# A replayed plan that knows of a shared port: new costs, three ways for V's parts, and a new order table in an attention and feed-forward kernel

## The chip, the cores and the metric

One core of a Trainium2 chip runs the whole program in one launch. TensorE (PE) multiplies; its weight loads run beside it (PEld). VectorE (DVE), ScalarE (ACT) and GpSimd (POOL) do the elementwise work, and SyncE (SP) issues the DMAs. The metric is the device time of one execution in microseconds (us).

## The reference

```python
q, k, v: (8, 8, 576, 64) f32          # batch, heads, tokens, head dimension
scores = q @ k.T / sqrt(64)
scores = where(scores >= max(scores) - tau, scores, -1e9)      # row by row
attn = exp(scores - max); attn = attn / (sum(attn) + 1e-9)
x = (attn @ v) -> (4608 tokens, 512)
h = x @ w_in                                                  # (512, 2048)
g = where(h >= 1, h, where(h <= -1, 0, (h + 1)**2 / 4))
out = g @ w_out                                               # (2048, 512)
```

The kernel is given float64 weights and float32 q, k and v. Most products are made in f16 with each operand split in a high and a low part (hi and lo, where lo is the value less hi), so three products stand for one.

## The kernel before

**What is computed where.** Q, K and V come with the head dimension first, two heads of a batch (a pair) in one buffer. The 4608 query rows are cut into 288 tiles of 128 rows. A tile goes through this chain: scores on PE (L1073, two PSUM buffers s; the table PAIR says whether two tiles' products are issued together, J, or one tile after the other, S), row minimum on DVE (smax, L1127), exp on ACT (sexp, L1137), mask and row sum on DVE (smask, L1151), reciprocal on DVE, then the normalised row in two f16 parts, and a transposing DMA from SP (send, L1213) into eT. The parts are made in one of the ways that the table TILE names by tile: P (the default: normalise on POOL L1169, hi on ACT L1177, lo on POOL L1180), N (normalise on ACT L1172), V (hi on ACT L1207, lo on DVE L1210) and S (from PSUM). Attention times V (av, L1299) gives x on PSUM, which ACT and DVE split.

**V, Q and K.** For V of batches 1 to 7, POOL writes the high part twice (hi, L728), DVE the low part (lo, L733), and SP sends it. Q and K of the first four pairs are used plainly in f32, the others are split: by P (POOL normalises, ACT hi, POOL lo) or D (ACT hi, DVE lo, L656), which the table QHOW names by pair. The scale of V in batch 0 is taken from Gram matrices on PE (SSQV "G"), in the other batches from sums of squares on ACT (L685).

**Weights.** 16 slices each of w_in and w_out are loaded (512 KB each), turned from float64 into float32 bits (fix, low and b2 on ACT, POOL and DVE: table SIGN), measured by Gram matrices on PE (L881), scaled and split (table CONV: A and G on ACT and POOL with the low part on POOL L933; D with the low part on DVE, rest2, L939; P and Q with two PE products and one eviction, diff, L942; M one product).

**FFN.** ffn1 (L466, ph<-x,WI) makes 512 columns of h in a PSUM buffer ph (three of them), ACT and DVE make g (relu, square, gate, ghi, glo), and ffn2 (L466, acc<-WO,..) adds into the one buffer acc.

**What sets the order.** Each operation is put into a list with its engine and a cost in us written out by hand. ORDER is a table of 5016 numbers, the places of those operations in a replay (Plan.order): it gives each a time by its engine, its inputs (HOP is the time from one engine to another) and its buffers, and the operations are then issued by these times. So the table and the costs set the order in which each engine's queue stands; nothing is moved when the program runs. Where the replay leaves PE without work for over 0.4 us before 120 us, fillers are put in: products of ones into a PSUM bank that is free (keep_warm, L1454), for 75% of the gap.

Of the kernel before, what the change touches and what calls it, by code (L numbers as in the profile page):

```python
# [14 lines left out]
ALU = mybir.AluOpType  # L15
# [24 lines left out]
SEND, VSEND = (1.24, 0.2, 2.1), (1.7, 0.5, 2.5)  # L40
ORDER = [
# [219 lines left out]
class Op:  # L261
    def __init__(self, eng, cost, fn, work, mode):
        self.eng, self.cost, self.fn, self.work, self.mode = eng, cost, fn, work, mode
        self.take, self.uses, self.next, self.behind = [], [], [], []
        self.gives = None


class Plan:


    HOP = {"PE": 0.21, "DVE": 0.16, "ACT": 0.17, "POOL": 0.1, "SP": 0.08}
    FREE, QUEUE, TURN, PAUSE = 0.18, 6.5, 0.097, (3.4, 2.2)
# [56 lines left out]
    def order(self):  # L329
# [3 lines left out]
        for o in self.ops:  # L333
            o.t = 0.0
# [1176 lines left out]
```

## Time and profile before

| | |
|---|---|
| time, median of 3 runs (lowest to highest) | 1097.77 us (1097.62 to 1098.02) |
| span of the profiled execution | 1097.3 us |
| PE, DVE, ACT, POOL busy | 1073.0, 906.1, 871.2, 759.4 us |
| granted clock of PE, mean of the span | 0.993 |

The span runs from the first to the last instruction on the core; what the runs show beyond it is about 0.5 us. Busy is the time in which at least one instruction of an engine runs. The clock is a share of 2.4 GHz. An instruction's duration contains about 0.07 us that lies under the instruction before it where a queue runs without a gap.

### The profile page before, as it was taken

The page shows a single profiled execution, that of the slowest core. Times are in us where ns is not written, and L with a number is a line of the kernel's source. Part 1 is how long each engine was busy: PE and PEld are TensorE (multiplying, and loading weights), DVE is VectorE, ACT ScalarE, POOL GpSimd, SP SyncE. Part 2 cuts the span into 40 slices and gives each one's busy share as a digit, 9 for nine tenths or more (in the row PEclk, how much of TensorE's full clock was granted, in tenths as well). Part 3 has the DMA queues.
Part 4 walks back from the last instruction along what each step waited for, and adds up shares of the span by engine and source line. Part 5 has one row for each costly group of instructions (what it writes and reads, how often), then busy time and mean ns, then how long its engine had stood idle before and what let it go on. Part 6 is the DMA issues. An engine that isn't in the chain of part 4 may idle for free.

```text
span 1097.3 us, 36713 instructions
## 1 busy us (share of the span) xinstructions
PE 1073.0 (98%) x14591; PEld 790.6 (72%) x14591; DVE 906.1 (83%) x2651; ACT 871.2 (79%) x1682; POOL 759.4 (69%) x880
## 2 busy tenths in 40 slices
PE   8799999999999999999999999999999999999998
PEld 7477668777777777776777677777786677767774
DVE  5899999999888888988898998888887899877223
ACT  5999989897888897887798888778788986776333
POOL 5999998786678785897668776576567885565000
PEclk9799999999999999999999999999999999999999
DMA  9997899775977887787778788569856676557000
GB/s 352 332 256 143 139 188 141 152 140 115 191 140 141 152 152 127 135 150 137 139 142 146 150 128 147 113 127 164 151 102 120 131 128 127 105 95 132 18 15 20
DMA packets 420668, 155.88 MB, mean 142 GB/s; under 512 B 399504, under 2 KB 399504, under 8 KB 420496
## 3 DMA queue, kind: packets, MB, share of 16 engines
q1 hardware_dynamic: 420416, 153.41, 71.7%
q8 instruction: 114, 1.87, 0.7%
q14 instruction: 58, 0.48, 0.2%
q10 hardware_dynamic: 80, 0.13, 0.0%
HBM read 45.09 MB, written 9.44 MB: 50 GB/s over the span
## 4 chain that ended last, share of the span: by engine, by line
PE 80%; DVE 10%; DMA 5%; POOL 2%; issue 2%; ACT 1%; SPq 0%; DVEq 0%; POOLq 0%; ACTq 0%
PE acc L466 30%; PE ph L466 30%; PE s L1073 9%; PE ph L1299 9%; DMA eT<-hl 2%; DVE s L1127 2%; DVE e L1151 2%; POOL hl L1180 1%; PE ph L1454 1%; DMA qq<-in_q_dram 1%; DMA kk<-in_k_dram 1%; DMA raw<-in_v_dram 1%; DVE ph L1383 1%; POOL e L1169 0%; DVE WO L939 0%
## 5 line engine op out<-in xcount | busy, mean ns | idle before, releaser
L466 PEld LDWEIGHTS <-WI 128*64 128x64 f16 (+1 forms) x7446 | 407.3, 108 | 55.1 <-issue 18.3
L1180 POOL TENSOR_TENSOR hl<-e,hl 128x576 f16<-128x576 f32 x267 | 347.3, 1309 | 107.7 <-ACT hl L1177 101.8
L466 PE MATMUL ph<-x,WI 128*64 128x256 f16 (+1 forms) x6912 | 400.6, 264 | 2.3 <-DVE x L1311 0.9
L1169 POOL TENSOR_SCALAR e<-e,sm 128x576 f32<-128x576 f32 x259 | 203.5, 790 | 106.6 <-DVE sm L1161 75.3
L1151 DVE SCALAR_TENSOR_TENSOR e<-s,sm,e 128x578 f32<-128x578 f32 x286 | 229.9, 812 | 21.6 <-ACT e L1137 17.0
L1137 ACT ACTIVATE e<-s,sm 128x576 f32<-128x576 f32 x288 | 208.5, 739 | 40.4 <-DVE s L1127 36.4
L1127 DVE TENSOR_SCALAR_CACHE_REDUCE s<-s,pc 128x576 f32<-128x576 f32 x252 | 203.5, 820 | 36.6 <-PE s L1073 35.3
L1177 ACT ACTIVATE hl<-e 128x576 f16<-128x576 f32 x267 | 178.2, 680 | 44.1 <-POOL e L1169 41.1
L466 PE MATMUL acc<-WO,ga 128*64 128x512 f16 (+1 forms) x1590 | 203.4, 380 | 0.0
L1073 PE MATMUL s<-kk,qq 64*128 64x288 f16 (+3 forms) x1840 | 152.1, 300 | 9.9 <-DMA qq<-in_q_dram 5.2
L466 PEld LDWEIGHTS <-ga 128*64 128x64 f16 (+1 forms) x1590 | 91.2, 109 | 82.3 <-issue 9.9
L1383 DVE SCALAR_TENSOR_TENSOR ph<-ph,fcs,asq 128x512 f32<-128x512 f32 (+1 forms) x160 | 111.7, 700 | 46.1 <-ACT asq L1379 44.9
L1376 ACT ACTIVATE asq<-ph,fcs 128x512 f32<-128x512 f32 (+1 forms) x160 | 116.1, 736 | 37.7 <-PE ph L466 36.9
L1299 PE MATMUL ph<-eT,vst 128*64 128x320 f16 (+2 forms) x1928 | 122.7, 279 | 2.9 <-DMA eT<-hl 2.0
L1299 PEld LDWEIGHTS <-vst 128*64 128x64 f16 x1928 | 100.2, 110 | 22.9 <-issue 7.9
L1073 PEld LDWEIGHTS <-qq 64*128 64x128 f16 (+1 forms) x1680 | 66.2, 96 | 48.3 <-issue 35.6
L1388 ACT ACTIVATE ga<-ph,fcs 128x256 f16<-128x256 f32 (+1 forms) x160 | 70.2, 450 | 29.2 <-DVE ph L1383 22.4
L1379 ACT ACTIVATE asq<-asq 128x512 f32<-128x512 f32 x144 | 90.3, 629 | 3.2
L1393 DVE SCALAR_TENSOR_TENSOR ga<-ph,fcs,ga 128x256 f16<-128x256 f32 (+1 forms) x160 | 70.5, 449 | 23.7 <-ACT WI L1388 8.3
L466 PE MATMUL acc<-WO,gb 128*64 128x512 f16 (+1 forms) x546 | 71.0, 379 | 0.0
L466 PE MATMUL acc<-WO 128*64 128x512 f16 (+1 forms) x546 | 69.4, 380 | 0.0
L466 PE MATMUL acc<-WO,WI 128*64 128x512 f16 (+1 forms) x534 | 68.2, 380 | 0.0
(189 smaller groups left out, 1162.5 us busy)
## 6 DMA issues: line engine op xcount, KB each, us to landing
raw<-in_v_dram SPq DMA_DIRECT2D x32, 288.0 KB, 3.5
WO<-in_moe_w_in_dram SPq DMA_DIRECT2D x16, 512.0 KB, 8.6
out_dram<-ob SPq DMA_DIRECT2D x32, 256.0 KB, 2.8
raw<-in_q_dram SPq DMA_DIRECT2D x28, 288.0 KB, 3.4
raw<-in_k_dram SPq DMA_DIRECT2D x28, 288.0 KB, 3.5
x<-in_moe_w_out_dram SPq DMA_DIRECT2D x10, 512.0 KB, 7.0
eT<-hl SPq DMA_TRANSPOSE x288, 3.5
WO<-in_moe_w_out_dram SPq DMA_DIRECT2D x4, 512.0 KB, 4.3
```

Source lines behind the costliest of these rows:

```text
L466: T.matmul(out[x], lhsT[:, x], rhs, **flags)
L1073: T.matmul(ap(sb, s_ps)[r, f, :SH], q, k, start=ql == kl == 0, stop=exact or ql == 1)
L1127: V.tensor_scalar(sv(), sv(), c, None, ALU.mult, ALU.min, accum_out=t[:, 0:1])
L1137: A.activation(ev(), sv(), AF.Exp, bias=ap(m, sm)[:, 0:1], scale=-1.0)
L1151: V.scalar_tensor_tensor(ev(SH + 1), sv(SH + 1), t[:, 2:3], ev(SH + 1), ALU.is_le, ALU.mult, accum_out=t[:, 3:4])
L1169: G.tensor_scalar(ev(), ev(), ap(m, sm)[:, 5:6], ESC, ALU.mult, ALU.mult)
L1177: A.activation(part2(0), ev(), AF.Copy)
L1180: G.tensor_tensor(part2(w), ev(), part2(0), ALU.subtract)
L1299: T.matmul(o[hd * D : (hd + 1) * D, :n], vt[:, k, hd * D : (hd + 1) * D], t[:, kb, (hd ^ p % 2) * n : ((hd ^ p % 2) + 1) * n], start=m == ...
L1376: A.activation(tv()[:, :, c], hv()[:, :, c], AF.Relu, bias=fcs[:, b, 2, q : q + 1], scale=fcs[:, b, 3, q : q + 1])
L1379: A.activation(ap(tb, asq), ap(tb, asq), AF.Square)
L1383: V.scalar_tensor_tensor(hv()[:, :, c], hv()[:, :, c], fcs[:, b, 0, q : q + 1], tv()[:, :, c], ALU.max, ALU.min)
```

## The change

The replay gets other costs, a table of hop times by both engines, and one new rule: an operation marked port (the DVE low parts that read two operands from SBUF) and an operation on POOL can't be under way together in the replay. V's parts can be made in three ways by a table VHOW: G as before (24 of 28), A (hi on ACT from the raw values, lo on DVE, 2) and P (POOL normalises, hi on ACT, lo on POOL, 2). QHOW now names Q and K apart. The tables CONV, SIGN, THR, PAIR, TILE and ORDER (now 4992 numbers) are new. TILE has 33 tiles of way V instead of 19, 39 of N instead of 8, one of S instead of 2. PAIR has 8 S instead of 11 (those at places 18 and 31 of the table, whose Q and K are split, are J now). SSQV is "A" for batch 0 too. Diff on PE falls from 4 to 2. Fillers go to the bank that stays free longest, and the first gap gets half as many.

```diff
-CONV = {"i": "AGAGGAGGPAGAADDP", "o": "PDDAADMGAAQGAGAD"}
-SIGN = {"i": "NNNAADANAAANANAA", "o": "AAAANANAAANANNNN"}
+CONV = {"i": "AGAGDDGGPAAGADDA", "o": "PDDAADMGGADGAGAD"}
+SIGN = {"i": "NNNAAAANAAAAANAA", "o": "AANNAANAANNNANNN"}
+VHOW = "GGGGAGGGGGGGGGGGPGGGGPGAGGGG"
-SEND, VSEND = (1.24, 0.2, 2.1), (1.7, 0.5, 2.5)
+SEND, VSEND = (1.45, 0.2, 2.5), (1.9, 0.5, 2.9)
-    0, 605, 606, 607, 608, 609, 12, 16, 13, 17, 1, 14, 18, 15, 19, 20, 21, 590, 592, 22, 23, 595, 580, 582, 591, 585, 587, 2, 593, 600, 611, 616, 596,
...
-SSQV = "GAAAAAAA"
+SSQV = "AAAAAAAA"
...
+            if o.port and t + o.cost > busy[0]:
+                t = max(t, busy[1])
+            elif o.eng == "POOL" and t + o.cost > alone[0]:
+                t = max(t, alone[1])
             o.t = t
...
+            if o.port:
+                alone = t, end
+            elif o.eng == "POOL":
+                busy = t, end
...
-            o1 = plan.op("POOL", 1.197, hi, [so], take=[tb], uses=[rb])
-            o2 = plan.op("DVE", 1.2 if b == 1 else 1.1, lo, [o1], uses=[rb, tb])
+            for how in plan.ways(("v", 4 * b + p - 4), VHOW[4 * b + p - 4], "GAP"):
+                o = plan.op("POOL", 0.712, norm, [so], uses=[rb]) if how == "P" else so
+                o = plan.op(*(("POOL", 1.197) if how == "G" else ("ACT", 1.14 if how == "A" else 1.05)), partial(hi, how), [o], take=[tb], uses=[rb])
+                done.append(plan.op(*(("POOL", 1.25) if how == "P" else ("DVE", 0.615)), partial(lo, how), [o], uses=[rb, tb], port=how != "P"))
...
-                n = plan.op("DVE", 0.92, lo_v, [n], uses=[e, m, x])
+                n = plan.op("DVE", 0.615, lo_v, [n], uses=[e, m, x], port=True)
...
-            gap = WARM[2] * (o.t - free)
+            gap = WARM[2] * (o.t - free) * (0.5 if free < 3 else 1)
...
-                    until[p, x] = min([t0 for q, y, t0, t1 in plan.held if (q, y) == (p, x) and t1 > free] + [o.t])
+                    until[p, x] = min([t0 for q, y, t0, t1 in plan.held if (q, y) == (p, x) and t1 > free] + [1e9])
```

**What moves, three places.** First SP's loads at the start of the program. WO and x are staging places of weight slices (512 KB each), kk and qq the plain K and Q of a pair (288 KB each). Before:

```order
L571 DMA qq_81<-in_q_dram 128x576
L571 DMA kk_77<-in_k_dram 128x576
L839 DMA WO<-in_moe_w_in_dram 128x1024
L839 DMA x_107<-in_moe_w_out_dram 128x1024
L839 DMA x_105<-in_moe_w_out_dram 128x1024
L839 DMA WO<-in_moe_w_in_dram 128x1024 x3
L571 DMA kk_78<-in_k_dram 128x576
L571 DMA qq_82<-in_q_dram 128x576
```

After:

```order
L870 DMA WO<-in_moe_w_in_dram 128x1024 x3
L587 DMA qq_81<-in_q_dram 128x576
L870 DMA WO<-in_moe_w_in_dram 128x1024 x2
L587 DMA qq_82<-in_q_dram 128x576
L870 DMA x_105<-in_moe_w_out_dram 128x1024
L587 DMA kk_78<-in_k_dram 128x576
```

The later load of the third pair (kk_78, qq_82) stood behind 17 weight slices and 9 loads of Q, K and V; it stands behind 14 and 9 now.

Second PE at the same third pair: s are score buffers, acc<-WI a Gram matrix of weights, ph<-ones a filler. Before:

```order
L1454 LDWEIGHTS ones
L1454 MATMUL ph_65<-ones 128x128
L1073 MATMUL s_61<-kk_77,qq_81 128x288
L1073 MATMUL s_62<-kk_77,qq_81 128x288
L1073 MATMUL s_61<-kk_77,qq_81 128x288
L1073 MATMUL s_62<-kk_77,qq_81 128x288
L1073 MATMUL s_61<-kk_78,qq_82 128x288 x2
L1073 MATMUL s_62<-kk_78,qq_82 128x288 x2
L881 LDWEIGHTS WI
```

After:

```order
L1485 LDWEIGHTS ones
L1485 MATMUL ph_63<-ones 128x128
L1104 MATMUL s_61<-kk_78,qq_82 128x288 x2
L1104 MATMUL s_62<-kk_78,qq_82 128x288 x2
L912 LDWEIGHTS WI
L912 MATMUL acc<-WI 128x128
```

The scores of the third pair stood right behind those of the second; now one Gram matrix of weights (4 products) and 55 fillers stand between them.

Third DVE a little ahead of the fifth ffn2: L939 and L970 are rest2 (low part of a weight slice), L1210 and L1241 the low part of a tile of way V, L1151 the mask, L1127 and L1158 the row minimum. Before:

```order
L939 SCALAR_TENSOR_TENSOR WO<-WO,wsc_o 128x512
L1161 RECIPROCAL sm_126<-sm_126 128x1
L1127 TENSOR_SCALAR s_61,sm_125<-s_61,tcs 128x2x288
L1127 TENSOR_SCALAR s_62,sm_127<-s_62,tcs 128x2x288
L939 SCALAR_TENSOR_TENSOR WO<-WO,wsc_o 128x512
L1210 SCALAR_TENSOR_TENSOR hl_96<-e_91,sm_123,hl_96 128x576
L1151 SCALAR_TENSOR_TENSOR e_89,sm_125<-s_61,sm_125,e_89 128x578
```

After:

```order
L1241 SCALAR_TENSOR_TENSOR hl_96<-e_91,sm_122,hl_96 128x576
L1342 SCALAR_TENSOR_TENSOR x_103<-ph_63,x_103 128x128
L1414 SCALAR_TENSOR_TENSOR ph_65<-ph_65,fcs,asq_101 128x512
L970 SCALAR_TENSOR_TENSOR WO<-WO,wsc_o 128x512
L1158 TENSOR_SCALAR s_62,sm_126<-s_62,tcs 128x2x288
L1192 RECIPROCAL sm_124<-sm_124 128x1
L970 SCALAR_TENSOR_TENSOR WO<-WO,wsc_o 128x512
```

Two low parts with both operands in SBUF stood next to each other; in the new order other DVE work lies between them here.

Further down the PE queues are alike: the last 150 of some 710 operations on PE stand in the same order in both.

## Rows read from the trace of the kernel before

**Rows 1.** Windows: busy us of each engine (instructions), granted clock, DMA share, GB/s

```profile
20.00:30.00 10.00, 9.23 (x94) 7.01 (x91) 8.85 (x33) 8.64 (x16) 7.88 (x10) 1.00 1.02 399
30.00:40.00 10.00, 4.79 (x22) 3.12 (x20) 9.01 (x25) 9.93 (x19) 9.58 (x13) 0.69 1.21 392
40.00:50.00 10.00, 7.85 (x57) 5.76 (x54) 8.64 (x27) 9.77 (x17) 9.92 (x11) 0.67 1.03 238
...
20.00:143.50 123.50, 108.81 (x1251) 79.54 (x1247) 114.11 (x342) 115.22 (x225) 116.80 (x134) 0.94 0.96 228
...
1050.00:1100.00 50.00, 42.77 (x406) 27.43 (x401) 12.39 (x32) 17.67 (x41) 0.00 (x0) 0.96 0.05 17
sum 950.00, PE 940.46 PEld 691.50 DVE 778.42 ACT 740.60 POOL 627.59; mean PE 49.50 PEld 36.39 DVE 40.97 ACT 38.98 POOL 33.03
```

**Rows 2.** Timeline of PE: start, us, operation, [idle before and what ended it]

```profile
35.78 3.27 PE L1073 MATMUL s<-kk,qq 64*128 64x288 f32 x8 [5.21 <-DMA qq<-in_q_dram]
87.76 0.90 PE L1454 MATMUL acc<-ones 128*128 128x128 bf16 x13
...
124.81 1.02 PE L942 MATMUL ph<-WO,dgw 128*128 128x512 f32 x2
125.67 0.38 PE L943 MATMUL ph<-WO,minus 128*128 128x512 f16 x1
...
143.49 1.49 PE L466 MATMUL acc<-WO,ga 128*64 128x512 f16 x12
...
148.24 1.17 PE L1073 MATMUL s<-kk,qq 64*128 64x288 f16 x12
```

**Rows 3.** Timeline of PE between 156 and 162 us, scores of a pair issued together

```profile
160.65 0.91 PE L1073 MATMUL s<-kk,qq 64*128 64x288 f16 x12
```

**Rows 4.** Groups by form: busy us, mean ns (L1134: 20 to 143.5 us)

```profile
L939 DVE SCALAR_TENSOR_TENSOR WO<-WO,wsc_o 128x512 f16<-128x512 f32 x4 | 5.9, 1463 | 0.1
...
L656 DVE SCALAR_TENSOR_TENSOR kk<-raw,pc,kk 128x576 f16<-128x576 f32 x5 | 5.2, 1036 | 0.0
...
L939 DVE SCALAR_TENSOR_TENSOR WI<-WI,wsc_i 128x512 f16<-128x512 f32 x2 | 1.6, 804 | 0.0
...
L1134 DVE TENSOR_SCALAR sm<-sm,tcs 128x1 f32<-128x1 f32 x19 | 3.9, 212 | 0.6
...
L685 ACT ACTIVATE junk<-raw 128x576 f16<-128x576 f32 x28 | 19.2, 685 | 1.4 <-DMA raw<-in_v_dram 1.4
...
L685 ACT ACTIVATION_READ_ACCUMULATOR junk<-raw 128x1 f32 x28 | 5.6, 202 | 0.0
...
L649 ACT ACTIVATE qq<-raw,pc 128x576 f16<-128x576 f32 x5 | 3.9, 777 | 0.0
...
L645 POOL TENSOR_SCALAR raw<-raw,pc 128x576 f32<-128x576 f32 x46 | 34.0, 749 | 2.0
...
L933 POOL TENSOR_TENSOR WI<-WI 128x512 f16<-128x512 f32 x12 | 13.9, 1164 | 0.6 <-ACT WI L928 0.2
```

**Rows 5.** Timeline of POOL and of DVE around 105 us, a low part beside POOL

```profile
103.74 1.28 POOL L658 TENSOR_TENSOR qq<-raw,qq 128x576 f16<-128x576 f32 x1
105.01 1.17 POOL L1169 TENSOR_SCALAR e<-e,sm 128x576 f32<-128x576 f32 x1
...
104.10 1.47 DVE L939 SCALAR_TENSOR_TENSOR WO<-WO,wsc_o 128x512 f16<-128x512 f32 x1
105.49 1.29 DVE L1210 SCALAR_TENSOR_TENSOR hl<-e,sm,hl 128x576 f16<-128x576 f32 x1
```

**Rows 6.** Line statistics: duration in ns, least, median and most

```profile
L1210 DVE SCALAR_TENSOR_TENSOR hl<-e,sm,hl x19: 799/824/1803, 105.5 to 1009.3; 128x576 f16<-128x576 f32 x19
...
L1169 POOL TENSOR_SCALAR e<-e,sm x259: 740/751/1359, 30.1 to 1005.3; 128x576 f32<-128x576 f32 x130
```

**Rows 7.** Timeline of ACT in the first 16 us

```profile
9.85 0.63 ACT L853 ACTIVATE ph<-WO 128x512 f32<-128x512 f32 x1 [4.42 <-DMA WO<-in_moe_w_in_dram]
```

**Rows 8.** Waits between 20 and 143.5 us: in total, times, longest

```profile
PEld s L1073 <- DVE e L1151: 6.5, 10, 1.7
```

More of the change, by code (lines that the diff above doesn't have):

```diff
@@ L268 @@
 class Plan:
-    HOP = {"PE": 0.21, "DVE": 0.16, "ACT": 0.17, "POOL": 0.1, "SP": 0.08}
-    FREE, QUEUE, TURN, PAUSE = 0.18, 6.5, 0.097, (3.4, 2.2)
+    HOP = {
+        "PE": {"PE": 0.0, "DVE": 0.21, "ACT": 0.21, "POOL": 0.21, "SP": 0.21},
+        "DVE": {"PE": 0.15, "DVE": 0.14, "ACT": 0.17, "POOL": 0.24, "SP": 0.13},
+        "ACT": {"PE": 0.15, "DVE": 0.14, "ACT": 0.14, "POOL": 0.18, "SP": 0.14},
+        "POOL": {"PE": 0.08, "DVE": 0.08, "ACT": 0.06, "POOL": 0.12, "SP": 0.05},
+        "SP": {"PE": 0.12, "DVE": 0.08, "ACT": 0.05, "POOL": 0.08, "SP": 0.0},
+    }
+    FREE, QUEUE, TURN, PAUSE = 0.18, 6.5, 0.097, (3.4, 0.8)
     def __init__(self):
@@ L289, in join, with op @@
         return ops[0]
-    def op(self, eng, cost, fn, after=(), take=(), uses=(), work=None, behind=None, mode=0):
+    def op(self, eng, cost, fn, after=(), take=(), uses=(), work=None, behind=None, mode=0, port=False):
         o = Op(eng, cost, fn, work, mode)
+        o.port = port
         o.n = len(self.ops)
@@ L332, in order @@
         idle, dma, mode, self.held = dict.fromkeys(self.HOP, 0.0), 0.0, 0, []
+        busy, alone = (0.0, 0.0), (0.0, 0.0)
         for o in self.ops:
@@ L660, in add_qk @@
             o2, o3 = [], []
-            for how in plan.ways(("qk", at), QHOW[at], "PD"):
-                o1 = plan.op("POOL", 0.724, norm, [sc1], uses=[rb, cb]) if how == "P" else sc1
-                o2.append(plan.op("ACT", 0.582 if how == "P" else 0.67, partial(hi, how), [o1], take=[nb], uses=[rb, cb]))
-                o3.append(plan.op(*(("POOL", 1.245) if how == "P" else ("DVE", 0.8)), partial(lo, how), [o2[-1]], uses=[rb, nb, cb]))
+            for how in plan.ways(("qk", 2 * at + n), QHOW[2 * at + n], "PD"):
+                o1 = plan.op("POOL", 0.712, norm, [sc1], uses=[rb, cb]) if how == "P" else sc1
+                o2.append(plan.op("ACT", 0.573 if how == "P" else 0.666, partial(hi, how), [o1], take=[nb], uses=[rb, cb]))
+                o3.append(plan.op(*(("POOL", 1.25) if how == "P" else ("DVE", 0.615)), partial(lo, how), [o2[-1]], uses=[rb, nb, cb], port=how != "P"))
             o2, o3 = plan.join(o2), plan.join(o3)
@@ L707, in add_v @@
                 for p in range(NPAIR):
-                    o = plan.op("PE", 0.29, partial(gram, p), [loads[p], o], take=[] if p else [sb], uses=[bufs[p], sb])
+                    o = plan.op("PE", 0.487, partial(gram, p), [loads[p], o], take=[] if p else [sb], uses=[bufs[p], sb])
                 o = plan.op("DVE", 0.2, largest, [o], uses=[sb])
@@ L769, in lo @@
                     V.tensor_tensor(t[:r, nk + k0 : nk + k1], view()[:r, k0:k1], t[:r, k0:k1], ALU.subtract)
-                h = plan.op("ACT", (k1 - k0) * P / 1200 + 0.05, hi, [o], take=[] if k0 else [ob], uses=[tb, ob], behind=h)
+                h = plan.op("ACT", (k1 - k0) * P / 1200 + 0.062, hi, [o], take=[] if k0 else [ob], uses=[tb, ob], behind=h)
                 done.append(plan.op("DVE", (k1 - k0) * P / 960 + 0.065, lo, [h], uses=[tb, ob]))
@@ L804, in w_scale @@
         lg = plan.op("DVE", 0.2, largest, stats, uses=[gbuf])
-        ps = plan.op("PE", 0.1, sums, [lg, c_op], take=[sb])
+        ps = plan.op("PE", 0.05, sums, [lg, c_op], take=[sb])
         so = plan.op("DVE", 0.65, scales, [ps], uses=[sb])
@@ L908, in add_w @@
                 gbuf = plan.buf("acc")
-            stats.append(plan.op("PE", 0.243, gram, [o4], take=[gbuf] if not u else [], uses=[gbuf], behind=stats[-1] if stats else None))
+            stats.append(plan.op("PE", 0.232, gram, [o4], take=[gbuf] if not u else [], uses=[gbuf], behind=stats[-1] if stats else None))
         wscale[w] = []
@@ L974, in add_w @@
                     if how == "D":
-                        done.append(plan.op("DVE", 1.1, rest2, [o]))
+                        done.append(plan.op("DVE", 0.56, rest2, [o], port=True))
                         seen.append(done[-1])
@@ L1400, in attn_ffn_kernel @@
             me.append(o)
-            o = plan.op("ACT", 0.7 + 0.295 * (m - 1), relu, [o] + [fscale[b] for b in bs], take=[tb], uses=[hb])
-            o = plan.op("ACT", 0.53, square, [o], uses=[tb])
+            o = plan.op("ACT", 0.664 + 0.235 * (m - 1), relu, [o] + [fscale[b] for b in bs], take=[tb], uses=[hb])
+            o = plan.op("ACT", 0.527, square, [o], uses=[tb])
             o = plan.op("DVE", 0.665 + 0.263 * (m - 1), gate, [o], uses=[tb, hb])
```

92 lines of the change are left out of this document (52 added, 40 removed), and 400 rows, old and new, of the table ORDER.

## The prediction

> **What bounds the kernel now.** I read the windows first, since the busy shares of the whole span hide two stages. From 150 us to the end PE was idle for 9.5 of 950 us, and 7.2 of these lie in the last 50 us [rows 1]: up to 1050 us only 2.3 us of waiting are left in 900. PE bounds this stage, and only less work on PE or those 2.3 us can shorten it. The last 150 operations on PE stand in the same order in both kernels, so I leave the end alone.
>
> The stage before is another one. From 20 to 143.5 us DVE, ACT and POOL were busy for 114.1, 115.2 and 116.8 of 123.5 us, PE for 108.8, which holds fillers, at a granted clock of 0.94 [rows 1]. No engine has more than 9.4 us to spare there; PE has nominally 14.7 and, in truth, also what its fillers and its slow clock take. From 30 to 50 us the clock stood at 0.69 and 0.67, between the two levels, after PE had been busy for only 4.79 us of ten [rows 1]; the 12.64 us that PE worked there are some 8.6 us at the full clock, so 4.0 us were lost. In the same 20 us ACT was idle for 0.30 us and POOL for 0.50 us [rows 1]. So PE is idle and cold there behind two full engines, and a warmer PE alone brings little.
>
> The change must therefore be read at one point of equal progress: the start of the fifth ffn2 at 143.49 us [rows 2]. Counted in both orders, the same 34 exps, 34 row minima, 10 av, 8 ffn1 and 4 ffn2 stand before it. Nearly what this point moves is what the time moves.
>
> **The change, part by part, up to that point.** I counted the operations that stand before it on each engine, in both orders, and priced them with groups by form [rows 4].
>
> *DVE gets 2.9 us more.* Three more low parts of weight slices (rest2: two at 0.804 us, one at 1.463) make 3.07; two more low parts of Q and K at 1.036 make 2.07; three thresholds at 0.212 make 0.64 [rows 4]. Against that about 2.9 us leave: a tile of way S and a merge of sign bits become others' (1.5 us), one part of Q goes (0.67), small ones and steps that only stand later make the rest. Its idle time is 9.4 us, so 2.9 fit, if the idle places are where they are needed.
>
> *ACT gets 1.0 us less* after the first 15 us: it gains squares and high parts of Q and K (0.87 and two at 0.777 [rows 4]) and a normalisation (0.77), and loses high parts, three thresholds and parts of slices, 4.2 us together. I leave out 1.4 us of steps that merely stand later. The four sums of squares for V of batch 0 (0.685 and 0.202 each, 3.55 us [rows 4]) replace 20 Gram products on PE. They lie in the first 13 us, where ACT waited 4.42 us for a weight slice [rows 7]. That wait is their cover, and I cost them at nothing; if the loads of V come as late as the slice, the cover is gone and up to 3.55 us are added.
>
> *POOL gets about 3.5 us less* (up to 4.7 with steps that stand later): two normalisations at 0.749 (1.50), one high part of a slice at 1.16 [rows 4], one tile's normalisation at 0.75 [rows 6], and small steps. All told POOL loses 62 us in the program, but after 150 us this is idle time that costs nothing.
>
> *PE.* Diff falls from four to two; one takes 1.02 + 0.38 us, less what overlaps, 1.25 or so [rows 2], so 2.6 us of PE work go, in the stage where PE waits anyway: nothing. In PE's own stage two pairs of tiles with split Q and K (places 18 and 31 of PAIR) are issued together: 12 products one tile after the other took 1.17 us [rows 2], 12 together 0.91 [rows 3], so 2 x 0.26 = **0.5 us** off the bound. Of the 2.3 us of waiting after 150 us the new order may keep all or none; I take a third away, **0.8 us**, with 0 and 2.3 as ends.
>
> *The loads of the third pair.* PE waited 5.21 us for qq at 35.78 us [rows 2]. Three weight slices fewer stand ahead of that load: 3 x 512 KB = 1.57 MB at 399 GB/s [rows 1] is 3.9 us, so most of the wait goes. But 55 fillers and 4 Gram products now stand ahead of those scores; 13 fillers took 0.90 us [rows 2], 55 some 3.2 us net of overlap. If the load is in by then, they delay the scores by up to 1.9 us (3.2 less the 1.3 us by which the load may still be late). They keep the clock up, though. Since ACT and POOL are full in these 20 us, I cost this part at 0, between +1.9 and the 4.0 us of lost clock; neither end reaches further than the bounds of the three engines below.
>
> *The new port rule in the replay* moves only where steps stand. The trace shows its ground. A low part of a weight slice began on DVE at 104.10 us while POOL worked until 105.02, and took 1.47 us; the same form beside idle POOL took 0.80 [rows 4, 5]. POOL's normalisation right behind took 1.17 us instead of its median 0.751, and DVE's next low part 1.29 instead of 0.824 [rows 5, 6]. Four of rest2 at 1.46 us instead of 0.80 alone are 2.6 us of holding on DVE before the point. A clean order would give DVE these 2.6 back, which about cancels its 2.9 more.
>
> The Trainium skill ("SBUF — State Buffer", section "SBUF: two separate sides") says of this that VectorE and GpSimd share a pair of ports behind an exclusive lock: the instruction that starts first holds it to its end and the other blocks. The trace agrees, both ways round [rows 5]. The rule speaks against the change, for the change makes such low parts more numerous (83 instead of 63 in the program, 16 instead of 11 before the point). By it, holding that leaves DVE can come back on POOL.
>
> **The sum.** Which engine paces the stage decides. ACT and POOL are nearest to full. POOL gives 3.5. ACT gives 1.0, and of its idle time outside 20 to 30 us (8.3 - 1.4 = 6.9 us [rows 1]) I let a third go, since the replay plans holding and hops with better prices: 3.3. So I take **3.5 us** up to the point. The bounds are far apart: all of ACT's idle gone, 8.3 + 1.0 = 9.3 us; or DVE paces and keeps its waits, -2.9 us. Together 3.5 + 0.5 + 0.8 = 4.8 us. The profiled span is 1097.3 us, 0.5 under the median of 1097.77; with the same 0.5 around it: 1097.8 - 4.8 = **1093.0 us**.
>
> **The rivals.**
> *More: the three engines close up.* The early load lets PE hand over the third pair's scores in time, PE stays warm, and ACT runs almost without a gap: 9.3 + 0.5 = 9.8 us, 1088.0 us; with PE's 2.3 us of waiting gone too, 1085.7. For it: the wait of 5.21 us and the cold clock are the largest disturbance in the stage. Against it: ACT and POOL were 9.5 to 9.9 of 10 busy just there, though at 20 to 30 us they weren't [rows 1].
> *No change: the holding moves to POOL.* Five more two-operand low parts before the point, each able to hold POOL for its own 0.80 us [rows 4], are 4.0 us, which eats POOL's 3.5 to 4.7. The stage then ends where it did, and only the 0.5 us of the pairs stays, within what the order's small waits give or take: 1097.5 us. This is also what comes out if the new order doesn't keep the two apart on the chip because real times drift from planned ones. For it: the normalisation at 1.17 us [rows 5], and that the planned times are estimates by hand. Against it: POOL loses work throughout.
> *Slower: DVE becomes the bound.* DVE gets 2.9 us more, in the queue that also holds row minima and masks. With only two score buffers, a mask that stands behind a low part holds PE's next scores; weight loads for scores waited 6.5 us in ten places for such masks [rows 8]. If DVE's idle places (9.4 us) don't move with its work, the point comes 2.9 us later; if the three added rest2 are held as the worst were (1.47 us [rows 5], 1.3 us more than priced for two of them) and the two added low parts of Q and K lose as much as the tile at 1.29 did (0.47 each), 4.8 to 5.1 us later. Less the 0.5 us: 1100.2 to 1102, say 1101 us. It decides as soon as DVE's waits in the stage stay above 9.4 - 2.9 = 6.5 us. For it: DVE is the one engine that is given work. Against it: it has the holding of 2.6 us to win.
>
> **How the numbers follow.** The forecast (gain of 2.2 to 7 us, 1090.8 to 1095.6) has 0.45, the larger gain 0.17, no change 0.21, slower 0.17. A measurement of this kernel tells about 0.2%, 2.2 us, from no change. Faster is 0.45 + 0.17 = 0.62, same 0.21, slower 0.17. The range leaves out the best end of the larger gain and the worst of the slower case: 1086.5 to 1100.0.
>
> **What would show it.** The fifth ffn2 begins before 143.49 us, at about 140 (forecast), 134 to 136 (more), 143 (no change), 146 or later (slower). PE's window at 30 to 50 us: a clock near 1.00, and no wait of some us on qq; if it stays cold, my reading of the load is wrong. The low parts of slices and tiles should take near 0.80 us on DVE, and POOL's normalisations 0.75; a longer POOL at equal counts is the third case. From 150 to 1050 us PE's idle should stay under 2.3 us; several us there, behind DVE's masks or low parts of way V, would break the prediction, since I take that stage to be as full as it was. PE's whole busy time should fall, by the fillers and the diffs.

## The result: slower by 0.9%

The changed kernel takes 1108.34 us (median; 1105.68 to 1108.68 in four runs), the kernel before 1097.69 us beside it (1096.53 to 1098.02): ratio 1.0093, 95% interval 1.0079 to 1.0107. The forecast was 1093.0 us, its range ended at 1100.0. The profiled execution spans 1106.8 us instead of 1097.3, 9.5 more. In all executions whose span stands beside their time, of either kernel, the time lies 1.7 to 2.2 us over the span, not 0.5 as put ahead of the prediction; the profile of before thus shows one of its slower executions, and the differences between the two profiles come out about 1 us too small.

Windows of after, columns as in [rows 1] (busy us and instructions of PE, PEld, DVE, ACT, POOL; granted clock, DMA share, GB/s):

```profile
30.00:40.00 10.00, 6.12 (x71) 4.66 (x68) 9.66 (x29) 9.88 (x19) 9.88 (x10) 1.00 0.88 300
40.00:50.00 10.00, 8.60 (x54) 6.37 (x55) 8.00 (x23) 7.63 (x14) 8.95 (x13) 0.66 0.77 223
...
60.00:70.00 10.00, 10.00 (x116) 7.43 (x117) 7.32 (x22) 8.23 (x18) 8.45 (x11) 0.73 1.21 272
...
20.00:145.97 125.97, 109.30 (x1275) 80.42 (x1275) 115.13 (x338) 112.45 (x219) 114.92 (x125) 0.95 0.97 226
...
150.00:1050.00 900.00, 894.41 (x12549) 662.24 (x12547) 776.96 (x2300) 746.37 (x1422) 567.85 (x640) 1.00 0.73 132
```

The same long window of before, which [rows 1] gives only as part of a sum, reads:

```profile
150.00:1050.00 900.00, 897.69 (x12666) 664.07 (x12664) 766.04 (x2244) 722.93 (x1387) 627.59 (x692) 1.00 0.72 132
```

The timeline of PE in after (start, us, operation, idle before it and what ended that):

```profile
41.40 3.03 PE L1104 MATMUL s<-kk,qq 64*128 64x288 f32 x8 [4.11 <-DVE e L1182]
...
56.54 1.23 PE L1104 MATMUL s<-kk,qq 64*128 64x288 f32 x4 [2.60 <-DVE e L1182]
...
145.97 1.49 PE L482 MATMUL acc<-WO,ga 128*64 128x512 f16 x12
```

So 2.5 us are lost up to the fifth ffn2 (145.97 us, 143.49 before [rows 2]) and 7.1 us behind it. The second part sits in PE's own stage, at full clock in both kernels: in the 900 us of the long window PE is idle for 5.6 us (2.3 before), and it is less far on. All three other engines idle more before the point as well: of the 125.97 us from 20 us on DVE is idle for 10.8, ACT for 13.5, POOL for 11.1 us; before it was 9.4, 8.3 and 6.7 of 123.5 us [rows 1].

Over the whole span the busy times show where the moved work went. The page of after:

```profile
PE 1075.2 (97%) x14562; PEld 793.7 (72%) x14562; DVE 919.7 (83%) x2712; ACT 898.5 (81%) x1721; POOL 694.9 (63%) x813
```

The page of before:

```profile
PE 1073.0 (98%) x14591; PEld 790.6 (72%) x14591; DVE 906.1 (83%) x2651; ACT 871.2 (79%) x1682; POOL 759.4 (69%) x880
```

POOL lost 64.5 us; ACT got 27.3 and DVE 13.6. DVE and ACT hand PE its masks, exps and gates; POOL was the emptiest of the three.

**What PE waits for.** In the stage behind the start (165 to 1050 us) the waits of PE that the profile lists (us in total, times, longest) read in after:

```profile
PE s L1104 <- DVE e L1182: 2.4, 5, 1.0
PE ph L1330 <- DMA eT<-hl: 2.4, 6, 0.7
```

and in before:

```profile
PE ph L1299 <- DMA eT<-hl: 1.6, 3, 0.8
PE s L1073 <- DVE e L1151: 0.5, 2, 0.3
```

These listed waits are only a part of it. To see the whole, I took for every product of PE behind the point (143.49 and 145.97 us) the time to the start of the next one, less the idle time in between. Idle time grew from 2.3 to 5.6 us, of which 1.9 us of the growth stand in front of scores, 1.0 in front of av and the rest in front of ffn1. The products themselves follow each other more slowly: scores took 109.9 us instead of 107.9, ffn2 370.9 instead of 369.8, av 104.0 instead of 103.3, ffn1 about the same. So of the 7.1 us, 3.3 are idle time and 3.8 are slower products at full clock. What slows them isn't shown.

One wait for a mask in full, DVE, POOL and PE around 602 us in after:

```profile
601.37 1.14 DVE L761 SCALAR_TENSOR_TENSOR vb<-raw,scs,vb 128x576 f16<-128x576 f32 x1
602.43 0.81 DVE L1182 SCALAR_TENSOR_TENSOR e<-s,sm,e 128x578 f32<-128x578 f32 x1
...
601.16 0.74 POOL L661 TENSOR_SCALAR raw<-raw,pc 128x576 f32<-128x576 f32 x1
...
602.02 0.29 PE L1104 MATMUL s<-kk,qq 64*128 64x288 f16 x1
603.30 0.89 PE L1104 MATMUL s<-kk,qq 64*128 64x288 f16 x11 [0.99 <-DVE e L1182]
```

DVE's low part of V began while POOL normalised a raw tile, ran 0.3 us over its least time, the mask behind it began when it was done, and PE, whose score buffer that mask frees, stood for 0.99 us. The 0.3 us of holding are a third of that wait. Two more of the five mask waits stand behind a low part that ran over its least time:

```profile
431.60 1.85 DVE L1241 SCALAR_TENSOR_TENSOR hl<-e,sm,hl 128x576 f16<-128x576 f32 x1
...
435.29 0.89 PE L1104 MATMUL s<-kk,qq 64*128 64x288 f16 x11 [0.44 <-DVE e L1182]
...
500.37 1.56 DVE L761 SCALAR_TENSOR_TENSOR vb<-raw,scs,vb 128x576 f16<-128x576 f32 x1
...
503.46 0.89 PE L1104 MATMUL s<-kk,qq 64*128 64x288 f16 x11 [0.20 <-DVE e L1182]
```

The other two, 0.17 us at 359.94 and 0.63 us at 552.62, have no such low part in the 3 us of DVE's work before them. If the three waits shrank by all that their low parts ran over 0.80 us, at most 0.44 + 0.20 + 0.34 = 1.0 us would come back. So of the waits that the profile lists, holding right in front of a mask explains 1.0 us at most.

### The profile page after: what moved, and what is told of

Same layout as the page of the kernel before. It is cut to its first block, busy times and chain, and to the rows that moved or that the text cites. A ratio compares the mean times of both kernels' runs of the same rounds, so it can differ in the third digit from the quotient of the medians.

```text
span 1106.8 us, 36703 instructions
## 1 busy us (share of the span) xinstructions
PE 1075.2 (97%) x14562; PEld 793.7 (72%) x14562; DVE 919.7 (83%) x2712; ACT 898.5 (81%) x1721; POOL 694.9 (63%) x813
## 4 chain that ended last, share of the span: by engine, by line
PE 69%; DVE 11%; DMA 7%; ACT 4%; issue 4%; POOL 3%; SPq 1%; DVEq 0%; ACTq 0%; POOLq 0%
PE acc L482 26%; PE ph L482 26%; PE s L1104 8%; PE ph L1330 8%; DVE s L1158 3%; DMA eT<-hl 3%; DVE e L1182 2%; DMA x<-in_moe_w_out_dram 1%; POOL hl L1211 1%; DVE ph L1414 1%; ACT e L1168 1%; DVE hl L1241 1%; DMA kk<-in_k_dram 1%; DMA raw<-in_v_dram 1%; DMA WO<-in_moe_w_in_dram 1%
## 5 line engine op out<-in xcount | busy, mean ns | idle before, releaser
L1211 POOL TENSOR_TENSOR hl<-e,hl 128x576 f16<-128x576 f32 x254 | 330.0, 1308 | 133.7 <-ACT hl L1208 123.7
L1200 POOL TENSOR_SCALAR e<-e,sm 128x576 f32<-128x576 f32 x215 | 168.4, 788 | 123.0 <-DVE sm L1192 74.4
L1158 DVE TENSOR_SCALAR_CACHE_REDUCE s<-s,pc 128x576 f32<-128x576 f32 x252 | 202.2, 819 | 33.6 <-PE s L1104 33.1
L1208 ACT ACTIVATE hl<-e 128x576 f16<-128x576 f32 x254 | 169.6, 679 | 35.8 <-POOL e L1200 34.2
L1104 PE MATMUL s<-kk,qq 64*128 64x288 f16 (+3 forms) x1840 | 155.8, 299 | 12.7 <-DVE e L1182 11.4
L1330 PE MATMUL ph<-eT,vst 128*64 128x320 f16 (+2 forms) x1928 | 125.3, 282 | 4.5 <-DMA eT<-hl 3.7
L1330 PEld LDWEIGHTS <-vst 128*64 128x64 f16 x1928 | 102.9, 112 | 25.1 <-issue 12.1
L482 PE MATMUL acc<-WO,gb 128*64 128x512 f16 (+1 forms) x564 | 75.0, 380 | 0.0
L482 PE MATMUL acc<-WO 128*64 128x512 f16 (+1 forms) x510 | 64.5, 380 | 0.0
```

Source lines behind the costliest of these rows:

```text
L482: T.matmul(out[x], lhsT[:, x], rhs, **flags)
L1104: T.matmul(ap(sb, s_ps)[r, f, :SH], q, k, start=ql == kl == 0, stop=exact or ql == 1)
L1158: V.tensor_scalar(sv(), sv(), c, None, ALU.mult, ALU.min, accum_out=t[:, 0:1])
L1200: G.tensor_scalar(ev(), ev(), ap(m, sm)[:, 5:6], ESC, ALU.mult, ALU.mult)
L1208: A.activation(part2(0), ev(), AF.Copy)
L1211: G.tensor_tensor(part2(w), ev(), part2(0), ALU.subtract)
```

## Experiments

All times are medians, with the ratio to the kernel before and its 95% interval; the kernel before measured 1097.1 to 1097.9 us beside them. Distances in us are to 1108.34 and 1097.69. Each profile is of one execution, and the executions of one kernel differ by 0.5 to 6 us. "First wide ffn1" is the start of the first 64-column ffn1 (161.60 us before, 163.73 after), a second point of equal progress; what is left of the span behind it is "the rest" (935.7 before, 943.1 after, so 7.4 us more). The theory to test: the loss is DVE's work with two SBUF operands, which holds up POOL and is held up by it, in front of the masks. The rivals: the code (buffers, fillers) and not the order; the start; the planned prices. A further rival, that the 27.3 us which ACT got delay the chain, was not tested.

**1. The code without the order.** All old tables in the changed code:

```diff
-CONV, SIGN, THR, PAIR, VHOW, QHOW, TILE, ORDER, SSQV = (new)
+CONV, SIGN, THR, PAIR, QHOW, TILE, ORDER, SSQV = (old); VHOW = all "G"
```

The new prices, those of the transposing DMAs (SEND, VSEND) among them, stay. Each engine's operations stand in the same order as before, fillers aside.

> The changed code (prices of the replay, hop table, port rule, rule of the fillers) with all tables of the kernel before, ORDER among them. Theory: the loss of 10.6 us lies in the new tables, the order and the ways of tiles, and not in the rules of the replay, since the queue of each engine follows ORDER alone; then this runs as before, 1096.7 to 1098.7 us. Rival: the new rules cost time themselves, through the buffers that the replay hands out by its times and through the fillers; then it lies between 1100 and 1108 us.

1100.59 us, 1.0029 [1.0019, 1.0040]. With the old filler rule as well:

```diff
-gap = WARM[2] * (o.t - free) * (0.5 if free < 3 else 1)
+gap = WARM[2] * (o.t - free)
...
-... if (q, y) == (p, x) and t1 > free] + [1e9])
+... if (q, y) == (p, x) and t1 > free] + [o.t])
```

> The changed code with all old tables and the old rule of the fillers (bank and length). Theory: the changed rule puts fillers where they hold a bank or PE at the start; 1096.7 to 1098.7 us. Rival: the loss of 3 us lies in buffers behind 150 us, handed out by other prices; 1099.5 to 1102 us.

1098.81 us, 1.0012 [1.0002, 1.0021]. So with the old tables the code costs some 3 us (2.1 to 4.4 by the interval 1.0019 to 1.0040), of which the filler rule takes about 1.8 (the two intervals just touch). If the two parts add up, some 7.7 of the 10.6 us come with the new tables, that is with the new ways of making the parts and the new order together. The code's loss doesn't lie at the start: the first wide ffn1 begins at 160.95 us (161.60 before), and the rest takes 938.4 us, 2.7 more than before. PE idles there, in the long window for 5.1 us (2.3 before), although every engine has its old order:

```profile
150.00:1050.00 900.00, 894.93 (x12629) 665.47 (x12627) 764.49 (x2237) 721.87 (x1385) 626.67 (x691) 1.00 0.73 132
```

In the changed kernel the old filler rule gave nothing back:

> The changed kernel with the old rule of the fillers (bank and length). The order of each engine and all else stand as in the changed kernel; only fillers change. Theory: fillers stand in front of the scores of the third pair but don't set the time; 1106 to 1109 us. Rival: they cost the start its 2.5 us; 1104.5 to 1106 us.

1109.71 us, 1.0103 [1.0084, 1.0121].

**2. Start or rest.** Tables and ORDER spliced at the fifth ffn2: the new ones before it and the old ones behind, and the other way round.

> Every operation that stands ahead of the fifth ffn2 in the changed order, in that order, and behind it the order and the ways of the kernel before. Theory: there are two losses that have nothing to do with each other, 2.5 us up to the fifth ffn2 and about 7 us behind it. Then this takes 1097.7 + 2.5 = 1100.2 us (1099 to 1101.5), with the fifth ffn2 at about 146 us and PE's waits behind 150 us as few as before. Rival: the start leaves the later stage with too little in hand (tiles, parts of Q and K), so that the later waits come from the start; then 1104 to 1108 us.

1107.66 us, 1.0092 [1.0076, 1.0108]; first wide ffn1 at 170.31 us.

> The counterpart: the kernel before up to the fifth ffn2, and behind it the order and the ways of the changed kernel (16 more tiles of way V, 27 of way N). Theory of two losses: 1097.7 + 7 = 1104.7 us (1103.5 to 1106), fifth ffn2 at about 143.5 us. Rival, the later waits come from the start: 1098 to 1100 us.

1112.56 us, 1.0139 [1.0124, 1.0155]; first wide ffn1 at 168.65 us. Both totals missed the theory's ranges (the first lies in the rival's), and neither answers the question, since the seam (the place where one order is joined to the other) itself costs 6.6 and 7.0 us ahead of the first wide ffn1. The rest says more. All in the changed code, it takes 938.4 us with the old order throughout, 937.3 with the new start alone, 941.2 with the new order behind the point alone, and 943.1 with both. So of the 7.4 us, 2.7 come with the code, 2.8 to 5.8 with the new order (and ways) behind the point, and -1.1 to 1.9 with the start.

**3. The low parts cost less.** DVE's low parts of way V and of V (59 of the 83 two-operand ones) take half the columns; the other half of these low parts isn't computed. In the kernel before they are 47. The expectations count 57 and 43. Both kernels got the same edit.

```diff
-V.scalar_tensor_tensor(part2(w), ev(), ap(m, sm)[:, 5:6], part2(0), ...)
+V.scalar_tensor_tensor(part2(w)[:, 0], ev()[:, 0], ap(m, sm)[:, 5:6], part2(0)[:, 0], ...)
-V.scalar_tensor_tensor(t[:, 2 * S : 3 * S], ap(rb, raw), s[:, 2:3], t[:, :S], ...)
+V.scalar_tensor_tensor(t[:, 2 * S : 2 * S + SH], ap(rb, raw)[:, :SH], s[:, 2:3], t[:, :SH], ...)
```

> The changed kernel with the low parts of way V and of V made on DVE for 288 of their 576 columns alone (57 of the 83 two-operand low parts; the other half of each low part is left out, one extra memset of 576 columns stands in the first 7 us). The replay prices such a low part at 0.615 us; in the changed kernel one that nothing holds takes 0.72 us to the next start, and the mean is 0.87 (way V) and 1.08 (V), since POOL holds it. Theory A: the order was fitted to that price and is late because the low parts cost 0.25 to 0.46 us more each, on DVE in front of masks and minima; with half of the columns (0.36 us unheld, some 0.5 to 0.6 held) they cost what the replay thinks, and the changed kernel falls by 6 us or more, to 1102 us or under, with few waits of PE behind 150 us. Rival B: the low parts are not it; then it falls by less than 3 us, to 1105.5 or more.

> The kernel before with the same half of columns left out in its 43 such low parts: the control. Theory A: its order holds them at 0.92 to 1.2 us each and has room for them, and PE sets its pace behind 150 us, so it gains little, 1095 to 1098 us. Rival: it gains as much as the changed kernel does with its half; then the low parts are a burden of either order and don't explain the difference.

1102.86 us, 1.0047 [1.0032, 1.0062], and 1096.54, 0.9987 [0.9978, 0.9996]. Of the distance of 10.6 us 6.3 are left; the rest of the two differs by 2.5 us instead of 7.4. The other side of the same conflict, POOL's two-operand low part L1211 at half its columns (half of it isn't computed):

```diff
-G.tensor_tensor(part2(w), ev(), part2(0), ALU.subtract)
+G.tensor_tensor(part2(w)[:, 0], ev()[:, 0], part2(0)[:, 0], ALU.subtract)
```

> The changed kernel with POOL's low part of a tile (254 of them) made for 288 of 576 columns alone (the other half is left out; five memsets more in the first 7 us), so 0.65 us instead of 1.28. DVE's own work stays as it is; what falls is the time in which POOL can hold DVE's low parts. Theory A1: the extra time of DVE's low parts that matters is the holding by POOL; then the change gains some 4 to 6 us, as with half of DVE's low parts, 1102 to 1104.5 us, and the low parts of way V take some 0.85 us in the mean instead of 0.92. Theory A2: DVE's own time for 20 more low parts matters; then it gains under 2 us behind 150 us, 1106 to 1108 us.

> The kernel before with the same half of POOL's low parts left out: the control. POOL is one of the three full engines up to 143 us, so the start can gain some us in either kernel: 1092 to 1097 us. What counts is the difference to the same edit in the changed kernel: 10.6 us if POOL's holding and POOL's work are not what tells them apart, 5 or less if they are.

1098.50 us, 1.0013 [1.0003, 1.0023], and 1093.22, 0.9958 [0.9943, 0.9972]: 5.3 us of distance are left, and 2.6 in the rest. Both edits together:

> The changed kernel with half of the columns left out in DVE's low parts of way V and of V and in POOL's low parts of tiles (both edits together). Theory: the later loss is DVE's and POOL's low parts in each other's way; with both short, the waits of PE behind 150 us are gone, and what is left against the same edit in the kernel before is the start's 3 us: 1094 to 1096.5 us, 2.5 to 4 us above its control. Rival: the order itself is too tight behind 150 us; then the distance to the control stays at 5 us or more.

> The kernel before with both halves left out: the control. From its two single edits (-1.4 and -4.3 us) 1091 to 1094 us.

1093.32 us, 0.9956 [0.9941, 0.9971], and 1092.41, 0.9948 [0.9933, 0.9963]. The distance is **0.9 us** instead of 10.6, less than the 2.5 to 4 us that the theory left to the start: the first wide ffn1 comes 2.0 us later than in the control (159.32 and 157.28 us), and the rest is 1.4 us shorter (932.0 and 933.4). PE's waits from 165 to 1050 us, in the halved changed kernel and then in the halved kernel before:

```profile
PE ph L1332 <- DMA eT<-hl: 0.4, 1, 0.4
```

```profile
PE s L1075 <- DVE e L1153: 0.5, 2, 0.3
PE ph L1301 <- DMA eT<-hl: 0.2, 1, 0.2
```

POOL's edit takes away almost the same in both kernels (254 and 267 such steps [after and before] of 1.31 us, now 0.75), and rather more before; still the changed kernel won 9.8 us by it and the one before 4.5. So the loss goes when the low parts on DVE *and* POOL's beside them are short. That doesn't show that the two holding each other is its cause. The two edits together take 22 us of DVE's and 147 us of POOL's busy time (15 and 159 us in the kernel before), so they make room for any order that is too tight. And they took away the code's part too: the halved changed kernel still has the changed code, which alone made the rest 2.7 us longer, and its control hasn't. What the pages show of DVE under POOL's edit is small: 919.7 to 915.0 us busy in the changed kernel, 906.1 to 902.3 in the one before. The win thus isn't in shorter operations on DVE alone. That POOL's shorter link in the chain from exp to transpose gives slack to PE as well is an inference; no run separates the two. DVE's edit is less even: it shortens 59 operations in the changed kernel and 47 before, so 12 x 0.30 = 3.6 us of DVE work lie between the two kernels' wins of 5.5 and 1.2 us.

**4. Moving the conflict by hand.** 16 tiles of way V of the stage behind 150 us back to way P, whose low part is POOL's:

```diff
-TILE: V at places 45, 66, 77, 85, 113, 116, 148, 160, 164, 166, 167, 206, 208, 220, 224, 239
+TILE: P there
```

> The changed kernel with the 16 tiles behind the start that it alone makes in way V put back to way P (normalise on POOL, hi on ACT, lo on POOL), so that 16 low parts with two operands in SBUF leave DVE for POOL. Theory: PE's new waits for score buffers come from such low parts, which stand ahead of masks on DVE and are held by POOL there; then 3 to 5 us come back, 1103 to 1105.5 us, and the waits of some 0.6 to 1.2 us at 435 and 552 us are gone. Rival, the order behind the start is too tight wherever the low part is made: 1107 to 1110 us.

1114.60 us, 1.0152 [1.0135, 1.0169], 6 us worse than the changed kernel itself, and against the theory: DVE fell to 906.6 us busy, its value before, and yet the rest got 5 us longer. 16 of DVE's low parts moved behind the next mask in DVE's queue:

```diff
 DVE queue, at 16 places
-low part (12 of L761 and L1241, 4 of slices and Q); mask L1182
+mask L1182; low part
```

> The changed kernel with 16 of DVE's two-operand low parts moved behind the mask that stands one or two operations after them in DVE's queue; all else in its order. Theory: what costs is the place of the held low part in front of a mask that frees a score buffer; then 2 to 5 us come back, 1103 to 1106.5 us. Rival: the low part only holds something else up there (the send of its own tile, the next minimum), and the time stays or grows: 1107 to 1112 us.

1111.09 us, 1.0133 [1.0116, 1.0150]: slower again, and PE's waits for masks grew from 2.4 us in 5 places to 3.0 in 6. Both runs speak against the theory that a low part's place in front of a mask is what costs, and the first against DVE's amount of work alone. They don't settle it, since each such step by hand also moves buffers and all that is planned behind it.

**5. The price in the replay.** The replay plans a two-operand low part at 0.615 us (0.56 for a weight slice's). Prices as measured, same order, in the changed kernel and in the changed code with old tables:

```diff
-("DVE", 0.615), partial(lo, how)   -0.615, lo_v   -0.56, rest2
+("DVE", 1.06), partial(lo, how)    +0.87, lo_v    +0.93, rest2
```

> The changed kernel with the replay's prices of the two-operand low parts set to what they took in the mean in the changed kernel (0.87 to 1.06 us instead of 0.56 to 0.615), and of POOL's two tile steps to 0.76 and 1.28. ORDER stays, so each queue holds the same operations in the same order; only the buffers that the replay hands out, and some fillers, change. Theory: buffers handed out by wrong times cost some of the later loss; 1104 to 1107 us. Rival: buffers don't matter; 1107 to 1110 us.

> The changed code with all old tables and the same measured prices: the same order on every engine as in the kernel before. Theory: the 3 us that the changed code lost with the old tables (1100.6 us) come from buffers handed out by times with too cheap low parts; 1096.5 to 1098.5 us. Rival: they come from other prices or from the fillers; 1099.5 to 1102 us.

1109.57 us, 1.0103 [1.0088, 1.0118], and 1100.25, 1.0018 [1.0008, 1.0027] beside 1100.59 without. With the order fixed, the price sets only buffers and fillers. Better prices in that place gave nothing back in either kernel; so it isn't these prices through which the changed code loses its 3 us. Whether an order *made* with these prices would be better isn't shown.

**6. The start.** The kernel before with kk and qq of the third pair loaded ahead of three weight slices, the one part of the change on which the prediction chose 0:

```diff
 SP queue
-DMA WO<-in_moe_w_in_dram 128x1024 x3
-DMA kk_78, qq_82
+DMA kk_78, qq_82
+DMA WO<-in_moe_w_in_dram 128x1024 x3
```

> One part of the change alone: the kernel before with the loads of the third pair (K and Q) ahead of three weight slices on SP's queue. The prediction's step: the wait of 5.2 us on qq at 35.78 us falls to some 1.5 us or less, the clock from 30 to 50 us rises, and the time gains little, since ACT and POOL are full there: 1096 to 1098 us. Rival: the wait and the cold clock were on the path; then 1093.5 to 1095.5 us.

1103.62 us, 1.0059 [1.0042, 1.0076]: the early load, with what the replay plans anew around it, costs 6 us. PE's scores wait all the same, now for masks, and ACT's step on the low bits of a slice (L862) then waits for a bank behind PE (timelines of PE and ACT):

```profile
35.00 2.26 PE L1073 MATMUL s<-kk,qq 64*128 64x288 f32 x4 [4.71 <-DVE e L1151]
...
40.05 1.89 PE L881 MATMUL acc<-WI 128*128 128x128 bf16 x16
...
43.36 0.62 ACT L862 ACTIVATE ph<-WO 128x512 uint32<-128x512 uint32 x1 [4.79 <-PE ph L789]
```

Its trace also holds 324 fillers instead of 314, so the 6 us needn't be the load's alone. In the changed kernel the wait of 4.11 us at 41.40 us is of the same kind. DVE and POOL ahead of it:

```profile
37.59 1.78 DVE L970 SCALAR_TENSOR_TENSOR WI<-WI,wsc_i 128x512 f16<-128x512 f32 x1
39.29 0.15 DVE L490 TENSOR_SCALAR wsc_i<-ph 128x1 f32<-128x1 f32 x1
...
39.92 0.69 DVE L901 SCALAR_TENSOR_TENSOR WI<-WO,ph 128x512 uint32<-128x512 uint32 x1
40.53 0.81 DVE L1182 SCALAR_TENSOR_TENSOR e<-s,sm,e 128x578 f32<-128x578 f32 x1
...
41.27 0.81 DVE L1182 SCALAR_TENSOR_TENSOR e<-s,sm,e 128x578 f32<-128x578 f32 x1
...
37.73 1.35 ACT L1168 ACTIVATE e<-s,sm 128x576 f32<-128x576 f32 x2
...
37.54 1.28 POOL L1211 TENSOR_TENSOR hl<-e,hl 128x576 f16<-128x576 f32 x1
```

The exps were done at 39.08 us; the masks began 1.45 us later, behind a low part of a weight slice that POOL held until 38.82 (1.78 us instead of 0.80 [rows 4]), some small steps and a merge. With that low part and the merge moved behind the two masks:

```diff
 DVE queue
-L970 WI<-WI,wsc_i; L901 WI<-WO,ph; L1182; L1182
+L1182; L1182; L970 WI<-WI,wsc_i; L901 WI<-WO,ph
```

> The changed kernel with one low part of a weight slice (rest2, 1.78 us at 37.6 us, held by POOL) and one merge of sign bits taken from in front of two masks on DVE to behind them. In the changed kernel PE waited 4.1 us at 41.40 us for those masks. Theory: the wait falls to about 2 us, PE's clock stays nearer to full there, and 1 to 2.5 us of the start come back: 1106 to 1107.3 us. Rival: ACT and POOL are full there, and the start ends as late as before: 1108 to 1109 us.

1106.73 us, 1.0083 [1.0068, 1.0098]. The wait shrank to 2.69 us. The time is 1.6 us lower, as the theory has it, but the runs of the two overlap (1106.27 to 1107.98 us beside 1105.68 to 1108.68), so the gain isn't clear of noise. Last, 100 more fillers ahead of the scores at 41.40 and 56.54 us, to keep TensorE's clock up:

> The changed kernel with 60 fillers more on PE ahead of the scores that waited 4.1 us for two masks at 41.40 us, and 40 more ahead of those that waited 2.6 us at 56.54 us. In the changed kernel the clock was 0.66 from 40 to 50 us and 0.73 from 60 to 70 us, in the second of which PE was busy for all of the ten us. Theory: this cold clock lies on the path (DVE, ACT and POOL idle 1.6 to 2.7 us of ten there), unlike before; with PE kept busy the clock stays near 1.00 and 2 to 4 us come back, 1104.5 to 1106.5 us. Rival: the engines behind PE set the pace, and the clock costs nothing: 1107.5 to 1109.5 us.

1111.83 us, 1.0128 [1.0104, 1.0153]. It doesn't test the clock: the window from 60 to 70 us came back to 1.00, that from 40 to 50 us stayed at 0.67, and the fillers themselves waited for a PSUM bank (waits of PE):

```profile
PE ph L1485 <- DVE WI L901: 3.4, 1, 3.4
```

## Why the prediction was wrong, step by step

- **PE's stage: the step that failed most.** The sum let the change only gain there ("0 and 2.3 as ends") and counted the moved work up to the fifth ffn2 alone; behind it, it named only POOL's 62 us as "idle time that costs nothing". The 62 us were right (64.5), the conclusion wasn't: ACT (27.3 us) and DVE (13.6 us) got work, both stand right before PE, and this end of the stage had no loss in the sum. It also put the changed buffers and fillers at nothing without a reason; with the old order they alone made the rest 2.7 us longer. Measured: 0.8 us of gain became 7.1 us of loss. The prediction's last paragraph named the sign (several us of PE idle behind masks or low parts of way V), but no case carried it. Why PE loses there stays open in part, as said below.
- **The 3.5 us up to the point: wrong in sign.** POOL did get lighter there and so did ACT (116.80 to 114.92 and 115.22 to 112.45 us busy), but I let ACT's work and a third of its gaps turn into time, as if the fullest engine paced the stage alone. Instead every engine idles more, the point comes 2.5 us later, and PE's waits for masks grow from 2.0 us in 5 places to 8.9 in 6 up to the point (waits, before to 143.49 and after to 145.97 us):

```profile
PE s L1073 <- DVE e L1151: 2.0, 5, 1.0
```

```profile
PE s L1104 <- DVE e L1182: 8.9, 6, 4.1
```

  This points to the chain from exp through mask to scores, and not to the sum of any engine, as what paces the stage; the run that shortened one of these waits gained no more than the noise.
- **The load of the third pair: right on the wait, wrong on the price.** The 5.21 us for qq [rows 2] are gone; masks took their place, 4.11 and 2.60 us. I bounded the step by +1.9 and -4.0 us; in a run of its own it measured +6, with the buffers and fillers that move with it. The clock went from 0.69 and 0.67 at 30 to 50 us [rows 1] to 1.00 and 0.66, with 0.73 now at 60 to 70 us: the cold stretch moved, which is half of what I looked for.
- **DVE +2.9 us up to the point:** 115.13 instead of 114.11 us busy, 1.0 more and not 2.9, in a stretch that is 2.5 us longer. What I did not count is the place: part of it stands in front of masks.
- **V's sums of squares on ACT at nothing:** no cost shows; ACT's first exp begins at 23.19 us instead of 25.19.
- **The port rule: the 2.6 us were not won back.** A weight slice's low part of WO fell from 1463 ns [rows 4] to 921 in the mean, but that of WI rose from 804 [rows 4] to 1135. By form in after, with the two groups of the rest of the program:

```profile
L1241 DVE SCALAR_TENSOR_TENSOR hl<-e,sm,hl 128x576 f16<-128x576 f32 x33 | 31.0, 941 | 3.4 <-ACT hl L1238 1.3 <-POOL e L1200 0.9 <-issue 0.9
L761 DVE SCALAR_TENSOR_TENSOR vb<-raw,scs,vb 128x576 f16<-128x576 f32 x26 | 28.7, 1104 | 0.2 <-POOL vb L750 0.2
...
L970 DVE SCALAR_TENSOR_TENSOR WO<-WO,wsc_o 128x512 f16<-128x512 f32 x5 | 4.6, 921 | 0.0
L970 DVE SCALAR_TENSOR_TENSOR WI<-WI,wsc_i 128x512 f16<-128x512 f32 x4 | 4.5, 1135 | 0.0
```

  Against a least time of 0.80 us, as in [rows 6], the two groups still take 0.94 and 1.10. Added up over all DVE low parts with two operands, the time beyond the shortest of each kind in the two traces is 17.6 us with 63 of them and 17.8 with 83. Ahead of the point, where the prediction counted on winning 2.6 us, it grew from 5.4 to 6.7 us. Behind the point, where most of the loss lies, it fell from 12.2 to 11.1 us. What grew there is the work itself: 67 such low parts took 64.6 us in all, 52 took 53.7.
- **The port lock** that the prediction cited from the Trainium skill ("SBUF — State Buffer", section "SBUF: two separate sides") agrees with the traces: the low part at 37.59 us starts under a POOL step that ends at 38.82, and ends 0.55 us after it, at 39.37, with 1.78 us on its count. That holding comes back on POOL is borne out ahead of the point, with less than the 4.0 us of the rival "no change": POOL's two steps of a tile (normalisation and low part) took 3.2 us beyond their medians there instead of 1.8. Over the program it is 15.8 us in 469 steps instead of 17.3 in 526, the same 0.03 us a step.
- **The 0.5 us of the two pairs** can't be told apart in 7 us of loss.
- **The rivals.** "Slower: DVE becomes the bound" (0.17) had the mechanism, masks behind low parts with two score buffers; but it ran only up to the fifth ffn2 and stopped at 1102. Behind the point stand 67 two-operand low parts instead of 52 (83 - 16 and 63 - 11), 10.9 us more of DVE work: the same mechanism should have been carried through that stage. The range ended at 1100.0 although the slower case, with its chance of 0.17, gave 1100.2 to 1102: not only its worst end but all of it lay outside.
- **A reading:** the window to 1100 us [rows 1] runs 2.7 us past the end of the span, so PE's idle time behind 1050 us was 4.5 us and not 7.2; nothing hangs on it.

**What is shown and what isn't.** Shown: with the old tables the changed code (prices, buffers, fillers) costs some 3 us, behind the start; the new order and ways behind the point make the rest 2.8 to 5.8 us longer (each from a single profile); and both losses are gone when DVE's and POOL's low parts are halved. Not shown: why. Holding right in front of masks explains at most 1.0 us of PE's listed waits, and holding behind the point didn't grow. The low parts' own 10.9 us, ACT's 27.3 us and an order that is simply tighter are left as rivals, since halving makes room for all of them. In the changed kernel with DVE's halves the weight slices' low parts, which stayed whole, were held longer than ever (WO 921 to 1134 ns, WI 1135 to 1234). Nor is shown why 16 tiles of way V given back to POOL made it worse. No version that computes everything beat the kernel before.

## What to carry to other kernels

Work taken from an idle engine isn't free where the engines that get it are those that the bound engine (here PE, which sets the pace) waits for: give every moved step a loss side in the stage of the bound engine, and follow it through the whole program. Give the changed buffers and fillers a loss side too: with the order unchanged they cost some 3 us here. Price a DVE operation with two SBUF operands by its measured mean beside a busy POOL (0.94 to 1.10 us here) rather than by its least (0.80); whether an order made with such prices gains wasn't run. In a tuned order a moved load (with the buffers and fillers that moved with it) or a seam cost 6 to 7 us here, so an early load must first be asked what its consumer waits for next.

## What was not expected of the hardware

- The time that DVE's two-operand operations are held beyond their least stayed the same over the program, 17.6 and 17.8 us, though there are 20 more of them and the order was made to keep them off POOL's steps.
- Fillers can stall: the added ones waited 3.4 us for a PSUM bank that DVE's merge was still to read.
- The kernel before and the changed code with all old tables run the same work in the same order; only buffers and fillers differ, and the times are 1097.69 and 1100.59 us.
